# Two pools of on-chip memory change places: the late results of the attention in front of the weights' low parts

## The chip, the cores and the metric

One Trainium2 chip, one core of it. The metric is the device time of one execution of the kernel, in microseconds (us). Matrix products run on TensorE (PE; its loads of the stationary operand are PEld), element by element work on VectorE (DVE), ScalarE (ACT) and GpSimd (POOL), and SyncE (SP) issues the transfers (DMA). The memory on the chip has 128 partitions; a tile lies at the same byte address in each of them, and an "address" below is this byte offset within a partition.

## The reference

The inputs are q, k and v of shape (8 batches, 8 heads, 576 positions, 64), a feature matrix w_phi (64 x 128), and two weight matrices, w_in (512 x 2048) and w_out (2048 x 512), which arrive as 64-bit floats.

```python
def phi(x):
    proj = np.einsum('bhsd,df->bhsf', x, w_phi)
    proj = proj - np.max(np.abs(proj), axis=-1, keepdims=True)
    return np.concatenate([np.exp(proj), np.exp(-proj)], axis=-1)
q_p, k_p = phi(q), phi(k)
kv  = np.einsum('bhsf,bhsd->bhfd', k_p, v);  z = np.sum(k_p, axis=2)
num = np.einsum('bhsf,bhfd->bhsd', q_p, kv)
den = np.einsum('bhsf,bhf->bhs', q_p, z)[..., None] + 1e-06
x = num / den                      # laid out as 4608 tokens x 512
h = x @ w_in
out = (h - np.tanh(h)) @ w_out
```

A linear attention is followed by a two-layer network on its 4608 x 512 result.

## The kernel before, in words

**First stage, the attention (to about 344 us).** 32 units, one for each pair of heads of a batch, go through a software pipeline that is written out by hand in `period(i)`; the order in the text is the order on each engine. A unit's features are projected on PE, centred on DVE, exponentiated on ACT, and multiplied on PE again. Its last steps, the numerators `d` (L343, ACT), the denominators `dd` (L348, ACT), `dn`, their reciprocals `rn`, and the reciprocals spread over the partitions again, `rb` (L364), are the tiles of the pool `tail`. They reach each other by small DMAs (L354, L361, L366), POOL multiplies `d` by `rb` (L370), and L373 stores the product to DRAM as `xs`. Beside this, one 64-bit weight tile is decoded in each period to 32 bits on DVE (L183), into a tile of the pool `wpool`.

**The split of the weights.** The network is computed with products of the type fp32r, and each operand is split in a high and a low part so that three products replace one exact one. `split_w` (L83) copies a decoded weight tile to its high part (L90 or L92; tiles `whi`, `who` in the pools `wpa` and `wp`) and POOL writes the rest, the low part, to a tile of `wpool` (L96; tiles `wli`, `wlo`). So `wpool` is a ring of 34 buffers of 2048 bytes through which the decoded weights pass and in which the 32 low parts then stay to the end. The attention's result is split in the same way into `xh` and `xl` (L117, L118), the hidden layer into `gh` and `gl` (L566, L567).

**Second stage, the network (from about 344 us).** 9 groups of 512 tokens times 16 slices of the hidden layer are 144 steps. `stage1` (L530) makes 12 products into one PSUM tile, for each of 4 row blocks three (L538), named by moving and stationary operand: `xh` with `whi`, `xl` with `whi`, `xh` with `wli`. ACT and DVE then compute h - tanh(h) (L545 to L560). `stage2` (L570), two steps later, makes for each of 4 token blocks the product of moving `who` with stationary `gh` (L573) and of moving `wlo` with stationary `gh` (L574), and at last four products of moving `who` with stationary `gl` (L576). All 24 products of a step are 128 x 128 by 128 x 512. The order of the work is the order in which the step loop (L592) writes it, with pins for the copies.

**Where tiles lie.** Pools are laid out one behind the other in the order in which they are opened. L74 opens `wpool`, L75 `tail`, L78 and L79 the pools `wpa` and `xp0`, which stay to the end; the attention's own pools and then those of the second stage follow behind. `wpool` takes 34 x 2048 = 69,632 bytes, `tail` 10,624.

Of the kernel before, what the change touches and what calls it, by code (L numbers as in the profile page):

```python
# [32 lines left out]
def tile_linear_attention_moe(  # L33
# [37 lines left out]
    nc.gpsimd.memset(bias_t[:, 1:2], PB2)  # L71
    nc.gpsimd.memset(bias_t[:, 2:3], -Y0)
    nc.gpsimd.memset(bias_t[:, 3:4], 1e-6)
    wpool = ctx.enter_context(tc.tile_pool(name="wpool", bufs=2 * NF + 2))  # L74
    tail = ctx.enter_context(tc.tile_pool(name="tail", bufs=2))  # L75
    xs = [dram.tile([NHP, P, PC], F32, name=f"xs{i}") for i in range(NBP)]

    wpa = ctx.enter_context(tc.tile_pool(name="wpa", bufs=1, reuse_waits="tile"))  # L78
# [602 lines left out]
```

## Time and profile before

| | |
|---|---|
| median of 3 runs | 1150.69 us (1150.51 to 1151.16) |
| the profiled execution's own time | 1149.65 us |
| its span, from first to last instruction | 1147.7 us |
| TensorE's granted clock, mean | 0.997 of full speed |
| PE busy, before and after 343.7 us | 323.38 of 343.70 us, 796.28 of 804.00 us |

The profile gives each engine's busy time, groups of equal instructions with their count and mean duration, and the instructions in order of time with their starts. A matrix product's end is modelled, and the products overlap: its "duration" of some 0.39 us is longer than the distance to the next one's start (some 0.23 us), which is what sets the rate. A product followed by a later start is given a longer duration, so the mean duration of a group follows the distance to the next start: a difference between two groups' means is read as the same difference between their distances.

### The profile page before, as it was taken

How to read it: one execution, taken by the hardware profiler on the slowest of the kernel's cores; microseconds unless marked ns; L12 is line 12 of the kernel's file. 1: busy time of each engine (PE TensorE's matmuls, PEld its weight loads, DVE VectorE, ACT ScalarE, POOL GpSimd, SP SyncE). 2: the span in 40 equal slices, each digit the busy share in tenths (PEclk: the TensorE clock that was granted, in tenths of full speed). 3: DMA queues.
4: the chain of work that ended last, by engine and by line, in shares of the span. 5: the costliest groups of instructions: out<-in, count | busy, mean ns of one | idle time of the engine just before them, and what ended most of it. 6: DMA issues, size and time to landing. Idle time of an engine off the chain costs nothing.

```text
span 1147.7 us, 18756 instructions
## 1 busy us (share of the span) xinstructions
PE 1119.7 (98%) x7008; PEld 873.9 (76%) x7008; DVE 837.0 (73%) x1172; ACT 777.2 (68%) x1486; POOL 433.1 (38%) x345
## 2 busy tenths in 40 slices
PE   7999999999989999999999999999999999999997
PEld 5666666666657888888888888888888888888885
DVE  5888888888868866767767767667676676766664
ACT  4787787777778766666666666666666666666664
POOL 3677776666634552322222222222222222222221
PEclk9999999999999999999999999999999999999999
DMA  4566666666731011111002002002002002000000
GB/s 156 175 195 205 204 206 204 200 197 208 216 118 48 1 38 37 37 36 44 1 5 70 1 1 74 1 1 74 1 1 74 1 1 73 1 1 32 6 1 38
DMA packets 51163, 85.46 MB, mean 74 GB/s; under 512 B 13312, under 2 KB 24960, under 8 KB 51072
## 3 DMA queue, kind: packets, MB, share of 16 engines
q1 hardware_dynamic: 50912, 84.20, 23.3%
q8 instruction: 55, 0.90, 0.3%
q14 instruction: 36, 0.29, 0.1%
q10 hardware_dynamic: 160, 0.07, 0.0%
HBM read 65.08 MB, written 19.02 MB: 73 GB/s over the span
## 4 chain that ended last, share of the span: by engine, by line
PE 88%; DVE 4%; ACT 3%; POOL 2%; DMA 2%; issue 1%; SPq 0%; POOLq 0%; DVEq 0%; ACTq 0%
PE ph L538 35%; PE po L574 11%; PE po L573 11%; PE po L576 11%; PE po L320 5%; PE pc L271 5%; PE pp L225 3%; PE ptt L250 2%; PE pu L334 2%; ACT qe L260 1%; PE pt L225 1%; DVE kv L313 1%; ACT qe L256 1%; DMA rr<-rn 1%; DVE wi L183 1%
## 5 line engine op out<-in xcount | busy, mean ns | idle before, releaser
L567 POOL TENSOR_TENSOR gl<-s,gh 128x512 fp32r<-128x512 f32 x144 | 186.7, 1297 | 566.7 <-ACT gh L566 557.9
L545 ACT ACTIVATE y<-ph 128x512 f32<-128x512 f32 x144 | 86.0, 597 | 264.9 <-PE ph L538 264.9
L554 DVE SCALAR_TENSOR_TENSOR s<-s,y 128x512 f32<-128x512 f32 x144 | 101.9, 708 | 197.9 <-ACT s L547 197.7
L538 PE MATMUL ph<-xh,wli 128*128 128x512 f32 x576 | 228.7, 397 | 0.0
L538 PE MATMUL ph<-xl,whi 128*128 128x512 f32 x576 | 228.1, 396 | 0.0
L574 PE MATMUL po<-wlo,gh 128*128 128x512 f32 x576 | 227.5, 395 | 0.0
L573 PE MATMUL po<-who,gh 128*128 128x512 f32 x576 | 224.0, 389 | 2.0 <-ACT gh L566 2.0
L538 PE MATMUL ph<-xh,whi 128*128 128x512 f32 x576 | 224.3, 389 | 0.0
L576 PE MATMUL po<-who,gl 128*128 128x512 f32 x576 | 153.9, 389 | 0.0
L560 DVE COPY_PREDICATED s<-mk,th 128x512 f32<-128x512 uint32 x128 | 123.0, 961 | 13.1
L538 PEld LDWEIGHTS ph<-xh,whi 128*128 128x128 f32 x576 | 110.0, 191 | 25.4 <-issue 0.5
L573 PEld LDWEIGHTS po<-who,gh 128*128 128x128 f32 x576 | 108.7, 189 | 26.5 <-ACT gh L566 3.2
L574 PEld LDWEIGHTS po<-wlo,gh 128*128 128x128 f32 x576 | 107.8, 187 | 25.7
L538 PEld LDWEIGHTS ph<-xl,whi 128*128 128x128 f32 x576 | 108.1, 188 | 24.1
L576 PEld LDWEIGHTS po<-who,gl 128*128 128x128 f32 x576 | 108.0, 188 | 23.6
L538 PEld LDWEIGHTS ph<-xh,wli 128*128 128x128 f32 x576 | 108.1, 188 | 22.4
L547 ACT ACTIVATE s<-y,bias_t 128x512 f32<-128x512 f32 x144 | 104.7, 727 | 0.4 <-POOL gl L567 0.4
L553 ACT ACTIVATE mk<-y,bias_t 128x512 f32<-128x512 f32 x144 | 103.9, 722 | 1.4 <-DVE s L560 1.4
L557 DVE SCALAR_TENSOR_TENSOR s<-s,ph 128x512 f32<-128x512 f32 x144 | 98.9, 687 | 5.2
L265 ACT ACTIVATE kp<-t 128x1024 f32<-128x1024 f32 (+1 forms) x128 | 86.9, 727 | 23.1 <-DVE t L236 21.2
L556 DVE SCALAR_TENSOR_TENSOR s<-s,s 128x512 f32<-128x512 f32 x128 | 88.9, 694 | 15.8 <-ACT s L549 3.5
L549 ACT ACTIVATE s<-y,bias_t 128x512 f32<-128x512 f32 x128 | 92.6, 723 | 0.9 <-POOL gl L567 0.9
(91 smaller groups left out, 1700.3 us busy)
## 6 DMA issues: line engine op xcount, KB each, us to landing
qk<-in_qkT SPq DMA_DIRECT2D x31, 576.0 KB, 5.2
v<-in_v SPq DMA_DIRECT2D x32, 320.0 KB, 3.2
rb<-rr SPq DMA_DIRECT2D x64, 144.0 KB, 3.3
xs<-rb SPq DMA_DIRECT2D x32, 288.0 KB, 3.6
out<-o SPq DMA_DIRECT2D x36, 256.0 KB, 2.0
rawi<-in_moe_w_in SPq DMA_DIRECT2D x16, 512.0 KB, 3.9
rawo<-in_moe_w_out SPq DMA_DIRECT2D x16, 512.0 KB, 5.8
xl<-xs SPq DMA_DIRECT2D x24, 256.0 KB, 4.1
```

The source lines that it names most:

```text
L538: nc.tensor.matmul(h, wt[:, c * P : (c + 1) * P], x[:, c, 0:N], start=(i == 0), stop=(i == 3 * NCT - 1))
L547: nc.scalar.activation(s1, y, AF.Square, bias=bias_t[:, 0:1])
L549: nc.scalar.activation(s2, y, AF.Square, bias=bias_t[:, 1:2])
L553: nc.scalar.activation(mk, y, AF.Relu, bias=bias_t[:, 2:3])
L554: nc.vector.scalar_tensor_tensor(s1, s1, PC1, y, ALU.add, ALU.mult)
L556: nc.vector.scalar_tensor_tensor(gs, s2, PC2, s1, ALU.add, ALU.mult)
L557: nc.vector.scalar_tensor_tensor(gs, gs, PA, h, ALU.mult, ALU.mult)
L560: nc.vector.copy_predicated(gs, mk.bitcast(U32), hh)
L567: pin(nc.gpsimd.tensor_tensor(gl, gs, f32(gh), ALU.subtract))
L573: nc.tensor.matmul(po[t], a, wo[f][0], start=(f == 0), stop=False)
L574: nc.tensor.matmul(po[t], a, wo[f][1], start=False, stop=False)
L576: nc.tensor.matmul(po[t], gl[:, t * P : (t + 1) * P], wo[f][0], start=False, stop=(f == NF - 1))
```

## The change

```diff
     nc.gpsimd.memset(bias_t[:, 3:4], 1e-6)
+    tail = ctx.enter_context(tc.tile_pool(name="tail", bufs=2))
     wpool = ctx.enter_context(tc.tile_pool(name="wpool", bufs=2 * NF + 2))
-    tail = ctx.enter_context(tc.tile_pool(name="tail", bufs=2))
     xs = [dram.tile([NHP, P, PC], F32, name=f"xs{i}") for i in range(NBP)]
```

The pool `tail` is opened, and so laid out, in front of `wpool`. The instructions of each engine, their order, their operands by name and the semaphores they wait for are the same in both built programs; only the addresses of the tiles of these two pools differ:

| tiles | pool | address before | address after | moved by | before, modulo 512 | after, modulo 512 |
|---|---|---|---|---|---|---|
| decoded weights, `wli`, `wlo` | wpool | 17,056 to 86,687 | 27,680 to 97,311 | +10,624 = 83 x 128 | 160 | 32 |
| `d`, `dd`, `dn`, `rn`, `rb` | tail | 86,688 to 97,311 | 17,056 to 27,679 | -69,632 = 34 x 2048 | unchanged | unchanged |
| `whi`, `who` | wpa, wp | from 97,312 | the same | 0 | 32 | 32 |
| `xh`, `xl` | xp0, xp | from 125,984 | the same | 0 | 32 | 32 |
| `gh`, `gl` | gm | from 220,192 | the same | 0 | 32 | 32 |

Modulo 2048, `wli` and `wlo` stand at 672 before and at 1056 after, and the other operands of the second stage's products at 1056 in both.

## The prediction

> **What bounds the kernel now.** I read the page first, then the engines by stretch, then the groups of the second stage, and last the chain and single products in order of time. The page's chain of waits, by engine and then by line, says where the time is set:
>
> ```profile
> PE 88%; DVE 4%; ACT 3%; POOL 2%; DMA 2%; issue 1%; SPq 0%; POOLq 0%; DVEq 0%; ACTq 0%
> PE ph L538 35%; PE po L574 11%; PE po L573 11%; PE po L576 11%; PE po L320 5%; PE pc L271 5%; PE pp L225 3%; PE ptt L250 2%; PE pu L334 2%; ACT qe L260 1%; PE pt L225 1%; DVE kv L313 1%; ACT qe L256 1%; DMA rr<-rn 1%; DVE wi L183 1%
> ```
>
> The four lines of the second stage's products make 68% of the chain. In that stage PE never rests (busy us of PE, PEld, DVE, ACT, POOL, then the granted clock), while DVE and ACT have much to spare:
>
> ```profile
> 400.00:700.00 300.00, 300.00 (x1306) 245.62 (x1306) 209.96 (x298) 196.59 (x347) 83.13 (x63) 1.00 0.09 29
> ```
>
> The chain near the end of the stage shows the length of a step (start, length, how many products):
>
> ```profile
> 1099.88 0.91 PE po L576 x4
> 1100.79 2.77 PE ph L538 x12
> ...
> 1105.40 0.91 PE po L576 x4
> 1106.31 2.77 PE ph L538 x12
> ...
> 1110.92 0.91 PE po L576 x4
> ```
>
> A step is 5.52 us (1105.40 - 1099.88 and 1110.92 - 1105.40), and 144 steps are 144 x 5.52 = 794.9 us, nearly all of the 804 us after the attention. So what the change does to the time is, almost alone, what it does to the distance between two products on PE, times 24 x 144 = 3456.
>
> **The 24 products are not equally fast.** All have the same shape. The groups between 400 and 1118 us, mean ns as the last figure before the bar:
>
> ```profile
> L538 PE MATMUL ph<-xh,wli 128*128 128x512 f32 x521 | 206.8, 397 | 0.0
> L538 PE MATMUL ph<-xl,whi 128*128 128x512 f32 x521 | 206.3, 396 | 0.0
> L574 PE MATMUL po<-wlo,gh 128*128 128x512 f32 x520 | 205.4, 395 | 0.0
> L538 PE MATMUL ph<-xh,whi 128*128 128x512 f32 x521 | 202.7, 389 | 0.0
> L573 PE MATMUL po<-who,gh 128*128 128x512 f32 x520 | 201.9, 388 | 0.0
> ...
> L576 PE MATMUL po<-who,gl 128*128 128x512 f32 x520 | 138.9, 389 | 0.0
> ```
>
> The means follow the distance to the next start, so there are two classes about 7 ns apart. The chain's lengths give the distances: L576 has 0.91 / 4 = 0.2275 us, L538 2.77 / 12 = 0.2308, and the L573 and L574 between them (5.52 - 2.77 - 0.91) / 8 = 0.230. With 227 ns for a quick product and 234 for a slow one, L538 is 4 x 227 + 8 x 234 = 2780 ns and the pairs are 4 x (227 + 234) = 1844 ns, which fits.
>
> The slow class is striking: `wlo` moving, `wli` standing, and `xl` with `whi`, during which `wli` is loaded for the next product. A tile of `wpool` takes part in each of these 12 products of a step, and in none of the 12 quick products. The pool is just what the change moves, from 160 to 32 modulo 512, where the other operands stand.
>
> **The change part by part.** *Instructions, order, waits:* all the same, 0 us.
>
> *The five tiles of `tail`* move by 34 x 2048 bytes, so what remains of their addresses modulo any power of two up to 2048 stays. Their rows (min, median, max over the 32 units, which use two buffers in turn; last, the transfers to `rb`):
>
> ```profile
> L370 POOL TENSOR_TENSOR rb<-d,rb x32: 1409/1417/1917, 46.3 to 484.6; 128x576 f32<-128x576 f32 x32
> DMA to landing us min/median/max: 2.8/3.3/6.3
> ```
>
> Both buffers give a median near the minimum. I take 0. The bound: the chain holds `rr<-rn` at 1%, 11.5 us, at most four landings of the shortest length 2.8 us seen for its sister `rb`; if each moved by the 0.5 us between minimum and median above, 2 us either way.
>
> *The decoded weights in the first stage* are written by DVE and read by POOL:
>
> ```profile
> L183 DVE SCALAR_TENSOR_TENSOR wi<-rawi,pt x16: 677/678/681, 33.9 to 340.3; 128x512 uint32<-128x512 uint32 x16
> L96 POOL TENSOR_TENSOR wli<-wi,whi x16: 1278/1291/1755, 41.2 to 418.4; 128x512 fp32r<-128x512 f32 x16
> ```
>
> L183 spreads by 4 ns over 16 tiles at different places of the ring; 32 times 4 ns is 0.1 us either way. POOL's work here runs beside PE and has room. I take 0; if the cover were gone, the 13 ns from minimum to median times 32 would be 0.4 us.
>
> *The low parts as operands of PE* are the term that decides, and no row of before shows them at another remainder. I bound it from both sides. Below: all slow products become quick. By the groups' means that is 12 x 7 = 84 ns a step, 144 x 84 = 12.1 us; by the chain's lengths 5.52 - 24 x 0.2275 = 0.06 us a step, 8.6 us. Above: the quick products become slow as well, 12 x 7 x 144 = 12.1 us the other way. Neither is hidden by anything: PE has no idle time in the stage. Nor does another engine stop a gain: DVE, the busiest, has 209.96 us in 300 us, which is 54.3 steps, so 3.86 us a step against a PE of 5.44.
>
> Which value? The rows just after PE has waited decide it for me. The first step of the stage, and the next:
>
> ```profile
> 344.35 0.39 PE L538 MATMUL ph<-xh,wli 128*128 128x512 f32 x1
> 344.58 0.40 PE L538 MATMUL ph<-xh,whi 128*128 128x512 f32 x1
> 344.82 0.39 PE L538 MATMUL ph<-xl,whi 128*128 128x512 f32 x1
> 345.05 0.39 PE L538 MATMUL ph<-xh,wli 128*128 128x512 f32 x1
> ...
> 346.67 0.39 PE L538 MATMUL ph<-xh,whi 128*128 128x512 f32 x1
> 346.89 0.40 PE L538 MATMUL ph<-xl,whi 128*128 128x512 f32 x1
> 347.13 0.40 PE L538 MATMUL ph<-xh,wli 128*128 128x512 f32 x1
> ...
> 348.75 0.39 PE L538 MATMUL ph<-xh,whi 128*128 128x512 f32 x1
> ```
>
> In the first step the product with `wli` is a 0.39 and the one of `xh` with `whi` a 0.40, the reverse of what the groups say, at the same addresses. Yet nine products take 346.67 - 344.58 = 2.09 us there and 348.75 - 346.67 = 2.08 us in the next step. So the 7 ns is not a toll that an operand pays each time; the sum of three products stays while the shares change hands. That looks like a rhythm in which loads and products fall, of which the groups show the settled form, and I take the nearest row, the unchanged sum: 0 us for this term.
>
> The Trainium skill, "TensorE: Matmul & The Clock Gate", section "Step-by-step: what each phase is for", has PE reading through two independent ports, so that loading the next stationary tile takes no bandwidth from the running product; by that rule the place of a tile would not matter and the sum would be the same 0. The same page's section "Back-to-back issue gap" gives 512 / 2.4 + 2.5 = 216 ns for such a product, and this trace, with 227 to 234, shows 11 to 18 ns more that neither rule explains. So the page does not close the other cases.
>
> **The sum.** 0 + 0 + 0 + 0 on the profiled execution's own 1149.65 us (span 1147.7). The median of the runs is 1.04 us above it, so the forecast is 1150.7 us.
>
> **The rivals.** *Faster: the toll is real.* Slow products are slow because `wpool` stands at another remainder than what PE reads beside it; moved to the same one, they run like L576, where moving and stationary tile both stand at 32 modulo 512. For it: the split of the groups has no exception. Against it: the first step above. Its price is the lower bound, 8.6 to 12.1 us; with 11 us, 1139.7 us.
>
> *Slower: the quick products lose their pace.* If the pace comes from the rhythm, the pool's new place can upset it as well as help it. The place is the run of four at L576, the start of each step's stretch without low weights. In the settled state and after the wait near the end:
>
> ```profile
> 691.24 1.07 PE L576 MATMUL po<-who,gl 128*128 128x512 f32 x4
> 692.15 0.39 PE L538 MATMUL ph<-xh,whi 128*128 128x512 f32 x1
> ...
> 1134.81 1.08 PE L576 MATMUL po<-who,gl 128*128 128x512 f32 x4
> 1135.73 0.39 PE L573 MATMUL po<-who,gh 128*128 128x512 f32 x1
> ```
>
> The same four products take 0.91 us (692.15 - 691.24) and 0.92 us (1135.73 - 1134.81). For it: the pace of the run can be lost without a change of operands. Against it: in the other rows of the chain it always comes back. If each of the four takes 7 ns more for good, 4 x 7 x 144 = 4.0 us, 1154.7 us; if the eight others follow, 1162.8 us. With PE full it decides from the first nanosecond, and by 2.3 us / 144 = 16 ns a step it can be told from no change.
>
> *That the change does not do what it says* is excluded by the addresses of the built program, which differ as listed.
>
> **How the numbers follow.** What a measurement here can tell from no change is about 0.2%, 2.3 us. No change has 0.47: the order is the same, the sums of the first step speak for it, and so do the unchanged remainders of `tail`; alone its range is 1149.5 to 1152. Faster has 0.34, for the split without exception. Slower has 0.19, of which about 0.07 for the small form at L576. The range goes down to the whole of the faster case, 1150.7 - 12.1 = 1138.6, and up to the small form of the slower one, 1154.7. Left out are the 0.12 of the large slower form and some edges of the cases, under 0.2.
>
> **What would show it.** Right: the chain's step stays 5.52 us, L538 x12 2.77, L576 x4 0.91, and the six groups keep their two classes. Faster: L574 and the two slow groups of L538 go from 395 to 397 towards 389, x12 towards 2.72, the step towards 5.44. Slower: L576 x4 rises towards 0.94 and the step over 5.54. The zero for `tail` is wrong if L370 or the landings of `rb` leave their medians of 1417 ns and 3.3 us, or if the second stage starts more than 2 us away from 343.8. The forecast as a whole is wrong if the step changes by 16 ns or more.

## The result

The changed kernel takes 1140.09 us (median of 5 runs, 1139.70 to 1143.24) where the kernel before, measured beside it, takes 1150.51 us (5 runs, 1150.36 to 1151.16). The ratio is 0.9911, with a 95% interval from 0.9899 to 0.9922: faster by 0.9%, 10.4 us. The forecast was 1150.7 us, no change, and it was wrong; the time lies in its range (1138.6 to 1154.7), near the number of the rival "the toll is real" (1139.7).

The six groups of the second stage's products in the changed kernel, between 400 and 1111 us:

```profile
L573 PE MATMUL po<-who,gh 128*128 128x512 f32 x524 | 203.8, 389 | 0.0
L574 PE MATMUL po<-wlo,gh 128*128 128x512 f32 x524 | 203.8, 389 | 0.0
L538 PE MATMUL ph<-xh,whi 128*128 128x512 f32 x522 | 203.1, 389 | 0.0
L538 PE MATMUL ph<-xl,whi 128*128 128x512 f32 x522 | 203.1, 389 | 0.0
L538 PE MATMUL ph<-xh,wli 128*128 128x512 f32 x522 | 203.1, 389 | 0.0
L576 PE MATMUL po<-who,gl 128*128 128x512 f32 x524 | 140.0, 389 | 0.0
```

The two classes are gone: the three groups at 395 to 397 ns have come down to 389, and the others stayed. The chain of waits of the changed kernel shows the steps (start, length, how many products):

```profile
1098.11 0.91 PE po L576 x4
1099.01 2.72 PE ph L538 x12
...
1103.55 0.91 PE po L576 x4
1104.45 2.72 PE ph L538 x12
...
1108.98 0.91 PE po L576 x4
```

L538's twelve take 2.72 us instead of 2.77, L576's four still 0.91, and a step is 5.44 us (1103.55 - 1098.11) instead of 5.52. 144 steps of 0.08 us are 11.5 us, a little more than the 10.4 us between the two medians.

The profiled execution of the changed kernel was its longest (1143.24 us, span 1141.1), and two other things in it hide part of the gain. Its second stage starts at 347.35 us instead of 343.78. In this execution the granted clock was 0.89 in the first 30 us where it was 0.94 before, and 0.57 between 341 and 345 us where it was 1.00. Over the fourteen profiles of this study that start lies anywhere from 343.3 to 347.4 us; the kernel below that moves only `gh` and `gl`, whose first stage has the addresses of the changed kernel's, starts its second stage at 345.27 us. So I count the late start to the execution, not to the layout. And near the end PE's clock falls again, which the last section shows. The second stage lasted 1141.1 - 347.35 = 793.8 us against 1147.7 - 343.78 = 803.9.

### The profile page after: what moved, and what is told of

Same layout as the page of the kernel before. It is cut to its first block, busy times and chain, and to the rows that moved or that the text cites. A ratio compares the mean times of both kernels' runs of the same rounds, so it can differ in the third digit from the quotient of the medians.

```text
span 1141.1 us, 18756 instructions
## 1 busy us (share of the span) xinstructions
PE 1113.4 (98%) x7008; PEld 876.0 (77%) x7008; DVE 837.1 (73%) x1172; ACT 777.7 (68%) x1486; POOL 432.5 (38%) x345
## 4 chain that ended last, share of the span: by engine, by line
PE 88%; DVE 4%; ACT 4%; POOL 2%; DMA 2%; issue 1%; SPq 0%; POOLq 0%; DVEq 0%
PE ph L538 34%; PE po L573 11%; PE po L574 11%; PE po L576 11%; PE po L320 5%; PE pc L271 5%; PE pp L225 3%; PE ptt L250 2%; PE pu L334 2%; ACT qe L260 1%; PE pt L225 1%; DVE kv L313 1%; ACT qe L256 1%; DMA rr<-rn 1%; DVE wi L183 1%
## 5 line engine op out<-in xcount | busy, mean ns | idle before, releaser
L573 PE MATMUL po<-who,gh 128*128 128x512 f32 x576 | 224.8, 390 | 1.8 <-ACT gh L566 1.8
L574 PE MATMUL po<-wlo,gh 128*128 128x512 f32 x576 | 224.7, 390 | 0.0
L538 PE MATMUL ph<-xh,whi 128*128 128x512 f32 x576 | 224.3, 389 | 0.1
L538 PE MATMUL ph<-xl,whi 128*128 128x512 f32 x576 | 224.1, 389 | 0.0
L538 PE MATMUL ph<-xh,wli 128*128 128x512 f32 x576 | 224.1, 389 | 0.0
L576 PE MATMUL po<-who,gl 128*128 128x512 f32 x576 | 154.6, 390 | 0.0
L573 PEld LDWEIGHTS po<-who,gh 128*128 128x128 f32 x576 | 108.4, 188 | 25.1 <-ACT gh L566 2.6
L538 PEld LDWEIGHTS ph<-xh,whi 128*128 128x128 f32 x576 | 108.3, 188 | 23.4 <-DVE s L560 0.5
L576 PEld LDWEIGHTS po<-who,gl 128*128 128x128 f32 x576 | 108.6, 189 | 22.6
L538 PEld LDWEIGHTS ph<-xh,wli 128*128 128x128 f32 x576 | 108.1, 188 | 22.5
L538 PEld LDWEIGHTS ph<-xl,whi 128*128 128x128 f32 x576 | 108.1, 188 | 22.2
```

What stands on the lines that cost most here:

```text
L538: nc.tensor.matmul(h, wt[:, c * P : (c + 1) * P], x[:, c, 0:N], start=(i == 0), stop=(i == 3 * NCT - 1))
L573: nc.tensor.matmul(po[t], a, wo[f][0], start=(f == 0), stop=False)
L574: nc.tensor.matmul(po[t], a, wo[f][1], start=False, stop=False)
L576: nc.tensor.matmul(po[t], gl[:, t * P : (t + 1) * P], wo[f][0], start=False, stop=(f == NF - 1))
```

## The experiments

Three theories were tested. **Distance:** a product is slow when its moving tile and a stationary tile that it holds, or that is loaded beside it, stand at different remainders. **Own address:** a tile is slow because of where it stands itself. **Rhythm:** loads and products fall in a beat, and any new layout may give any beat. The experiments add bytes that nothing uses between pools; all of them leave each engine's instructions, their order and their waits as they are, and compute everything. Below, "distance" is taken modulo 256 bytes.

### Moving both pools, keeping all distances

```diff
+    ctx.enter_context(tc.tile_pool(name="pad", bufs=1)).tile([P, 96], F32, name="pad")
     wpool = ctx.enter_context(tc.tile_pool(name="wpool", bufs=2 * NF + 2))
     tail = ctx.enter_context(tc.tile_pool(name="tail", bufs=2))
```

> The order of before (the weights' low parts first, the late results behind them), with 384 unused bytes in front of both: the low parts stand at 32 modulo 512, where they stand after the change, and all other operands of the network move along to 416, so every distance between two tiles is that of before. Distance theory (a product is slow when its moving tile and a stationary tile that it holds or that is loaded beside it stand at different remainders): step 5.52 us, 12 slow groups members as before, time 1150 us. Own-address theory (a tile is slow because of where it stands itself, 160 modulo 512 being bad and 32 good): the low parts are cured, step 5.44 us, 1140 us, unless 416 is bad too. Rhythm theory (any new layout may settle in any rhythm): anything from 5.44 to 5.60 us.

Measured: 1150.63 us, ratio to before 1.0001 (0.9991 to 1.0011). The groups of this kernel, between 400 and 1111 us, are those of before:

```profile
L538 PE MATMUL ph<-xh,wli 128*128 128x512 f32 x516 | 204.9, 397 | 0.0
L538 PE MATMUL ph<-xl,whi 128*128 128x512 f32 x516 | 204.3, 396 | 0.0
L574 PE MATMUL po<-wlo,gh 128*128 128x512 f32 x516 | 203.8, 395 | 0.0
L538 PE MATMUL ph<-xh,whi 128*128 128x512 f32 x516 | 200.7, 389 | 0.0
L573 PE MATMUL po<-who,gh 128*128 128x512 f32 x516 | 200.3, 388 | 0.0
L576 PE MATMUL po<-who,gl 128*128 128x512 f32 x513 | 137.1, 389 | 0.0
```

The low parts stand at 32 modulo 512, as after the change, and nothing is gained; the others stand at 416, and their groups are no slower. So the place 32 does not cure the low parts by itself, which excludes the own-address theory in its plain form, and this move did not shake the beat. Distance foretold just this; rhythm, which allows any value, is not excluded by it.

### Keeping the low parts, moving all others

```diff
     wpool = ctx.enter_context(tc.tile_pool(name="wpool", bufs=2 * NF + 2))
+    ctx.enter_context(tc.tile_pool(name="pad", bufs=1)).tile([P, 32], F32, name="pad")
     tail = ctx.enter_context(tc.tile_pool(name="tail", bufs=2))
```

> The order of before, with 128 unused bytes behind the pool of the low parts: these do not move (160 modulo 512), and all the other operands move to 160 as well. Distance theory: step 5.44 us, all six groups at 389 ns, time 1140 us. Own-address theory: the low parts stay slow, step at least 5.52 us, and with all operands at 160 up to 5.60 us, 1150 to 1162 us. Rhythm theory: anything from 5.44 to 5.60 us.

Measured: 1139.88 us, ratio 0.9904 (0.9889 to 0.9918). The chain of this kernel:

```profile
905.58 0.91 PE po L576 x4
906.49 2.72 PE ph L538 x12
...
911.02 0.91 PE po L576 x4
```

The step is 5.44 us. The old order of the pools, with its low parts where they were, gives all of the gain once the others stand at the same remainder. The order of the two pools is not the cause; it was a way to set the distance to 0.

### How far apart is the same?

```diff
     wpool = ctx.enter_context(tc.tile_pool(name="wpool", bufs=2 * NF + 2))     # the changed kernel
+    ctx.enter_context(tc.tile_pool(name="pad", bufs=1)).tile([P, 64], F32, name="pad")    # 256 bytes; then 16: 64 bytes
     xs = [dram.tile([NHP, P, PC], F32, name=f"xs{i}") for i in range(NBP)]
```

> The changed kernel with 256 unused bytes behind the pool of the low parts: they stay at 32 modulo 512, the other operands go to 288. Distance theory with a period of 256 bytes: step 5.44 us, nothing changes, 1140 us. With a period of 512 bytes or more: low and other operands differ, step 5.52 us, 1150 us. Own-address theory: the low parts are where they were, so 5.44 us if 288 is good.

Measured: 1140.48 us, ratio 0.9908 (0.9889 to 0.9928). The chain of this kernel keeps the step of 5.44 us (910.37 - 904.93):

```profile
904.93 0.91 PE po L576 x4
905.84 2.72 PE ph L538 x12
...
910.37 0.91 PE po L576 x4
```

> The changed kernel with 64 unused bytes behind the pool of the low parts: they stay at 32 modulo 512, the other operands go to 96, a quarter of 256. Distance theory, a matter of equal or not: step 5.52 us, 1150 us. Distance theory, a matter of overlap: something between 5.44 and 5.52 us. If only steps of 128 bytes count: 5.44 us. Own-address theory: 5.44 us if 96 is as good as 32.

Measured: 1154.26 us, ratio to before 1.0033 (1.0021 to 1.0045), so slower than before by 0.3%. The groups of the 64-byte kernel:

```profile
L538 PE MATMUL ph<-xh,wli 128*128 128x512 f32 x513 | 202.8, 395 | 0.0
L538 PE MATMUL ph<-xl,whi 128*128 128x512 f32 x514 | 202.4, 394 | 0.0
L574 PE MATMUL po<-wlo,gh 128*128 128x512 f32 x512 | 201.3, 393 | 0.0
L538 PE MATMUL ph<-xh,whi 128*128 128x512 f32 x514 | 200.8, 391 | 0.0
L573 PE MATMUL po<-who,gh 128*128 128x512 f32 x512 | 200.6, 392 | 0.0
L576 PE MATMUL po<-who,gl 128*128 128x512 f32 x513 | 139.9, 394 | 0.0
```

256 bytes apart counts as the same place, 64 does not, and before it was 128. None of the expected values came for the 64-byte kernel; the slowest of them was 1150 us. It also shows what distance alone does not say. L576, whose `who` and `gl` stand at one remainder, rises from 389 to 394, and its steps take 5.57 and 5.52 us in turn (909.53 - 903.96 and 915.05 - 909.53 in its chain), with the same distances in each. So a disturbed product seems to disturb the ones behind it, even into the next step, and the rhythm theory holds a part of the truth, below the distance.

### One of the two low weights right, the other wrong

```diff
-    wpool = ctx.enter_context(tc.tile_pool(name="wpool", bufs=2 * NF + 2))
+    wpi = ctx.enter_context(tc.tile_pool(name="wpi", bufs=NF + 1))
+    ctx.enter_context(tc.tile_pool(name="pad", bufs=1)).tile([P, 32], F32, name="pad")
+    wpo = ctx.enter_context(tc.tile_pool(name="wpo", bufs=NF + 1))
...
-        wl = wpool.tile([P, DM], F32R, tag="w", name=f"wl{nm}{f}")
+        wl = (wpi, wpo)[n % 2].tile([P, DM], F32R, tag="w", name=f"wl{nm}{f}")
...
-            w = wpool.tile([P, DM], F32, tag="w", name=f"w{u.nm}")
+            w = (wpi if u.nm[0] == "i" else wpo).tile([P, DM], F32, tag="w", name=f"w{u.nm}")
```

> The changed kernel with the pool of the low parts split in two, one for w_in and one for w_out, 128 unused bytes between them: wlo stands with all other operands at 160 modulo 512, wli alone at 32. Distance theory, by the groups of before: the two groups of L538 in which wli is held or loaded are slow (396 ns), L574 is cured (389 ns); 8 slow products a step, step 5.44 + 8 x 0.0067 = 5.493 us, time 1148 us. Rival, that any tile out of place upsets the whole rhythm: all groups between 389 and 397 ns, step near 5.52 us, 1151 us.

Measured: 1146.64 us, ratio to before 0.9966 (0.9950 to 0.9981). The groups of this kernel, between 400 and 1111 us:

```profile
L538 PE MATMUL ph<-xh,wli 128*128 128x512 f32 x519 | 206.0, 397 | 0.0
L538 PE MATMUL ph<-xl,whi 128*128 128x512 f32 x520 | 205.9, 396 | 0.0
L538 PE MATMUL ph<-xh,whi 128*128 128x512 f32 x520 | 202.3, 389 | 0.0
L573 PE MATMUL po<-who,gh 128*128 128x512 f32 x516 | 200.7, 389 | 0.0
L574 PE MATMUL po<-wlo,gh 128*128 128x512 f32 x516 | 200.7, 389 | 0.0
L576 PE MATMUL po<-who,gl 128*128 128x512 f32 x516 | 137.9, 389 | 0.0
```

`wlo`, put right, is cured alone; `wli`, wrong alone, slows the product that holds it and the one before, in which it is loaded. The step is 5.49 us, as worked out beforehand; the time is 1.4 us under the 1148 us expected. In this layout the toll can be counted product by product.

### The low weights right, gh and gl wrong

```diff
+        c2.enter_context(tc.tile_pool(name="pad", bufs=1)).tile([P, 32], F32, name="pad")
         gm = c2.enter_context(tc.tile_pool(name="gm", bufs=2, reuse_waits="tile"))
```

> The changed kernel with 128 unused bytes in front of the pool of gh and gl, so that the low weights stand right and gh and gl stand wrong (160 against 32). Distance theory: every product that holds or loads gh or gl is slow, which is all 12 of L573, L574 and L576 and the last of L538 in each step: step 5.44 + 13 x 0.0067 = 5.527 us, time 1152.6 us, L538's first two groups at 389 ns. Rival, that the low weights or their values are the cause: 5.44 us, 1140 us.

Measured: 1155.22 us, ratio to before 1.0035 (1.0022 to 1.0049). The groups of this kernel, between 400 and 1111 us:

```profile
L574 PE MATMUL po<-wlo,gh 128*128 128x512 f32 x514 | 203.5, 396 | 0.0
L573 PE MATMUL po<-who,gh 128*128 128x512 f32 x513 | 202.9, 396 | 0.0
L538 PE MATMUL ph<-xh,whi 128*128 128x512 f32 x512 | 201.8, 394 | 0.0
L538 PE MATMUL ph<-xh,wli 128*128 128x512 f32 x512 | 201.3, 393 | 0.0
L538 PE MATMUL ph<-xl,whi 128*128 128x512 f32 x512 | 198.9, 388 | 0.0
L576 PE MATMUL po<-who,gl 128*128 128x512 f32 x512 | 139.8, 394 | 0.0
```

Now products of high parts alone (L573) are slow, so it is neither the low parts' values nor their pool. The count was off: 13 slow products, a step of 5.53 us and 1152.6 us were expected, and the step is 5.55 us (911.39 - 905.84 in the chain). The L538 groups of `xh` are at 393 and 394, although their own tiles stand together, and only the last L538 product of a step loads a `gh` that stands apart. In the step that begins at 906.60 us, the first seven products of L538 behind L576 take 1.62 us (906.60 to 908.22), 231 ns each, and the next four 0.91 us, as quick ones do: the disturbance outlasts its cause by some seven products.

### All products at one distance other than 0

```diff
+    ctx.enter_context(tc.tile_pool(name="pad0", bufs=1)).tile([P, 32], F32, name="pad0")          # d bytes, here 128
     xp0 = ctx.enter_context(tc.tile_pool(name="xp0", bufs=1, reuse_waits="tile"))
...
+        c2.enter_context(tc.tile_pool(name="pad1", bufs=1)).tile([P, 32], F32, name="pad1")       # 256 - d
         wp.append(c2.enter_context(tc.tile_pool(name="wp", bufs=1, reuse_waits="tile")))
+        c2.enter_context(tc.tile_pool(name="pad2", bufs=1)).tile([P, 32], F32, name="pad2")       # 256 - d
         gm = c2.enter_context(tc.tile_pool(name="gm", bufs=2, reuse_waits="tile"))
```

> The changed kernel with unused bytes in front of the pools of xh and xl, of the late high weights and of gh and gl, so that in both stages every moving tile stands 128 bytes (modulo 256) from every stationary one. Distance theory, a matter of equal or not: all 24 products are slow, step 5.60 us, time 1163 us. Rival, that only a switch between distances costs (all equal, so no switch): 5.44 us, 1140 us.

> As the run with 128 bytes between all moving and all stationary tiles, but with a distance of +32 bytes (modulo 256): moving minus stationary is 32 in both stages. Distance theory, a matter of equal or not: step near 5.59 us as there, 1160 us. Graded theory (the two streams meet in the same part of the memory, and there may be a distance better than 0): anything from 5.3 to 5.6 us; under 5.44 us would be a version better than the change.

> The same with a distance of +64 bytes. Equal or not: 5.59 us, 1160 us. Graded theory: from 5.3 to 5.6 us, and not the value of +32.

> The same with a distance of +192, that is -64 bytes modulo 256. Equal or not: 5.59 us, 1160 us. Graded theory: from 5.3 to 5.6 us; the value of +64 if only the size of the distance counts, another if it matters which of the two streams is ahead.

> The same with a distance of +224, that is -32 bytes modulo 256. Equal or not: 5.59 us, 1160 us. Graded theory: from 5.3 to 5.6 us; the value of +32 if only the size of the distance counts, another if it matters which stream is ahead.

| moving minus stationary, modulo 256 | step, us | time, us | ratio to before (95%) |
|---|---|---|---|
| 0 (the change) | 5.44 | 1140.09 | 0.9911 (0.9899 to 0.9922) |
| +32 | 5.60 | 1161.06 | 1.0091 (1.0061 to 1.0120) |
| +64 | 5.52 | 1150.52 | 1.0001 (0.9989 to 1.0012) |
| 128 | 5.59 | 1160.24 | 1.0073 (1.0020 to 1.0127) |
| +192, or -64 | 5.59 | 1159.95 | 1.0081 (1.0052 to 1.0110) |
| +224, or -32 | 5.59 | 1159.06 | 1.0070 (1.0047 to 1.0093) |

The steps are read from the chains, as here for 128 and for +64 bytes (the first two rows and the last two):

```profile
905.62 0.93 PE po L576 x4
906.55 2.80 PE ph L538 x12
...
911.21 0.93 PE po L576 x4
```

```profile
902.03 0.91 PE po L576 x4
902.94 2.76 PE ph L538 x12
...
907.55 0.91 PE po L576 x4
```

At 128 nearly all 24 products are slow (24 x 234 ns would be 5.61 us, and 5.59 is measured), so it is not the switch between distances that costs. (All moving and stationary tiles of one stage stand at the distance named; at the two seams of a step, the tile that is loaded beside a product belongs to the other stage and stands otherwise.) The graded theory is right against "equal or not", since +64 costs half; and +64 differs from -64, so it matters which of the two streams is ahead. Of the six distances 0 is the best. None of these is a version that beats the change; the one with 128 bytes behind the low parts equals it.

The traces show one thing more. The starts of L576, averaged over the 126 to 130 steps of each trace between 400 and 1111 us, give a step of 5440.0 ns at distance 0 and of 5600.0, 5520.0, 5593.3, 5593.3 and 5586.7 ns in the rows below it. Each is longer than 5440.0 by a whole multiple of 6.67 ns: 24, 12, 23, 23 and 22 times, for 24 products. The kernel before has 12 (5520.0 ns), the one with `wli` alone apart 8 (5493.3), the one with `gh` and `gl` apart 17 (5553.3), and the 64-byte kernel 13 and 19 in its two kinds of step (5526.7 and 5566.7). So, summed over a step, the toll has one size in all these layouts, and what the distances change is how many tolls a step pays.

### The same distances from another start

```diff
+    ctx.enter_context(tc.tile_pool(name="pad", bufs=1)).tile([P, 8], F32, name="pad")
     tail = ctx.enter_context(tc.tile_pool(name="tail", bufs=2))
     wpool = ctx.enter_context(tc.tile_pool(name="wpool", bufs=2 * NF + 2))
```

> The changed kernel with 32 unused bytes in front of everything: all operands of the network stand at 64 modulo 512 where they stood at 32, all distances are kept. Distance theory: step 5.44 us, 1140 us. Rival, that the 11 to 13 ns by which even a quick product exceeds 512 columns at full clock come from starting at half of 64 bytes: the step falls below 5.44 us, at best to 24 x 0.216 = 5.18 us, 1103 us.

Measured: 1140.57 us, ratio 0.9900 (0.9866 to 0.9934), step 5.44 us. Whether all operands start at 32 or at 64 modulo 512 makes no difference. So the quick products' 227 ns do not come from starting at 32; what they are made of stays open.

## Why the prediction was wrong

**What held.** The bound was named rightly: the time changed by what PE's distance between products changed, times the steps, with no other engine in the way. The two classes of 12 products, with the low pool in each slow one, were the whole story, and the lower bound was sized well: 8.6 to 12.1 us by the two ways of reading, 11.5 by the steps now and 10.4 by the medians. The zeros of the first stage hold as well. In the changed kernel L370 and the landings of `rb` show

```profile
L370 POOL TENSOR_TENSOR rb<-d,rb x32: 1407/1418/1915, 48.5 to 486.4; 128x576 f32<-128x576 f32 x32
DMA to landing us min/median/max: 2.8/3.4/6.2
```

against medians of 1417 ns and 3.3 us. The second stage did start more than 2 us later, which I had named as a sign against these zeros; as the start scatters by 4 us over the profiles, and by 2 us between two kernels whose first stage has the same addresses, it is no sign.

**The step that failed** is the one under "Which value?", from the first rows after PE had waited to "the 7 ns is not a toll that an operand pays". It took those rows for the same state as the settled one with its shares exchanged. The changed kernel shows the same rows, where no operand stands apart. Its first step, in order of time:

```profile
347.69 0.39 PE L538 MATMUL ph<-xl,whi 128*128 128x512 f32 x1
...
348.15 0.40 PE L538 MATMUL ph<-xh,whi 128*128 128x512 f32 x1
...
348.61 0.40 PE L538 MATMUL ph<-xh,wli 128*128 128x512 f32 x1
348.85 0.39 PE L538 MATMUL ph<-xh,whi 128*128 128x512 f32 x1
...
350.89 0.39 PE L538 MATMUL ph<-xh,whi 128*128 128x512 f32 x1
```

The five products from 347.69 to 348.85 take 232 ns each; the nine from 348.85 to 350.89 take 227. So the first products behind a wait run at some 231 ns in both kernels, for a reason that no run shows and that does not need a tile standing apart. In the kernel before, three such products (693 ns) happen to last as long as one quick and two slow ones (227 + 234 + 234 = 695), and the equal sums that I trusted were this coincidence. Rows from a start were used to judge a settled state, against 3100 rows of the settled state itself that had no exception.

**The rivals.** "The toll is real" is what happened, by its mechanism too: the kernel whose pool of low parts did not move and that still gained, and the one in which it moved to no effect, show that the distance decides. "The quick products lose their pace" did not happen here, but the 64-byte kernel shows that it can: L576's four, with their own tiles at one remainder, take 0.93 us there instead of 0.91, and the time is 1154.26 us. The rival's price of 1154.7 us for the small form lies near that by chance, since in that kernel other groups change too. The kernels with `gh` and `gl` or all tiles 128 bytes apart (1155.22 and 1160.24 us) are not this rival; there L576's own tiles stand apart.

**The rule of the Trainium skill** ("TensorE: Matmul & The Clock Gate", "Step-by-step: what each phase is for"), that a load of the next stationary tile takes nothing from the running product because PE has two independent read ports, would have left the time at 1150 us in all these layouts. The measurements differ: the same products in the same order take from 5.44 to 5.60 us a step by the addresses of the two tiles alone. Here the measurement decides. The 216 ns that the prediction takes from the section "Back-to-back issue gap" of the same page of the Trainium skill are given there for an isolated product; for a stream of loads and products of 512 columns it gives about 131 ns. No kernel here comes near that: the quick products take 227 ns.

**What stays open.** Why 0 is best and +64 second is not explained, nor why a toll is 6.67 ns, nor why tolls go on behind a disturbed product. That reads of the two streams meet in the same part of the memory is a guess that would fit a period of 256 bytes; no run shows it. Nor is it told apart whether a product that holds `wli` pays for its own stationary tile or for the disturbance of the one before it, since the two always follow each other.

## What to carry to other kernels

When groups of products of one shape differ by a few ns, list what distinguishes them before calling it noise: here it was the pool of one operand, and an unused pad of 128 bytes was worth 1.0% (ratio 0.9904). Where PE is the bound with fp32r products of this form, 128 x 128 by 128 x 512 with a load for each, let moving and stationary tiles start at the same remainder modulo 256 bytes; other forms were not tried here. And look at the addresses again after any change in the size of a pool that lies in front of others. Judge a settled state by settled rows, not by the first ones after a wait.

## What was not expected of the hardware

The size of the whole span: from the best to the worst layout the network's step goes from 5.44 to 5.60 us and the time from 1140 to 1161 us, 1.8%, with the same instructions. And in the profiled execution of the changed kernel the granted clock falls to half after PE waited for 1.78 us near the end. Four windows of 1 us of that execution, with the clock as the third figure from the end:

```profile
1125.00:1126.00 1.00, 0.73 (x3) 0.65 (x4) 0.00 (x0) 0.74 (x2) 0.65 (x1) 1.00 0.00 0
1126.00:1127.00 1.00, 1.00 (x4) 0.76 (x4) 0.00 (x0) 0.33 (x1) 1.00 (x2) 0.59 0.00 0
1127.00:1128.00 1.00, 1.00 (x4) 0.81 (x3) 0.57 (x1) 0.40 (x1) 0.88 (x1) 0.50 0.00 0
1128.00:1129.00 1.00, 1.00 (x4) 0.71 (x3) 0.97 (x2) 0.00 (x0) 0.00 (x0) 0.50 0.00 0
```

The eleven products from there to the next step's first take 1129.71 - 1125.60 = 4.11 us where they took 1135.73 - 1133.20 = 2.53 us before, 1.6 us more. A wait of the same length stands at this place in the other profiles too (1.70 us before, 1.77 us in the second experiment), and the clock stayed up in those; why it fell in one execution is open.
